# Attention followed by a soft mixture of experts on one core: memory handed from attention to expert weights in eleven steps in place of six, load marks 20 entries later, and a newly written order

## Chip, cores and metric

The kernel runs on one core of a Trainium2 chip. The metric is device time in microseconds (us) of one execution; smaller is better. A stated time is the median of three runs.

## What is computed

All data are float32. The first half is a linear attention with a random-feature map, for 8 batches x 8 heads x 576 tokens of 64 values; the second half is a soft mixture of 8 experts with 4 slots each over the 4608 tokens of 512 values that the first half yields.

```
def phi(x):
    proj = einsum('bhsd,df->bhsf', x, w_phi)            # 64 -> 128 features
    proj = proj - max(abs(proj), axis=-1)
    return concatenate([exp(proj), exp(-proj)], axis=-1)
q_p, k_p = phi(q), phi(k)
kv  = einsum('bhsf,bhsd->bhfd', k_p, v);  z = k_p summed over s
attn = einsum('bhsf,bhfd->bhsd', q_p, kv) / (einsum('bhsf,bhf->bhs', q_p, z) + 1e-6)

x = attn as 4608 x 512;  logits = x @ phi               # 512 -> 32 slots
d = softmax of logits over the 4608 tokens;  slot_input = d.T @ x
slot_out[e] = relu(slot_input[e] @ w1[e]) @ w2[e]       # 512 -> 1024 -> 512, e = 0..7
out = (softmax of logits over the 32 slots) @ slot_out
```

The softmax over tokens needs the logits of every token, so the two expert layers can start only when all of attention is done; the last product needs the outputs of all experts.

## The kernel before, in words

**Stages.** Attention works on 32 head pairs (two batches of one head, 9 tiles of 128 tokens each) and, across them, on 72 blocks of four token tiles. For a block, `proj` multiplies the transposed keys and queries with the feature matrix on TensorE (tiles psk and psq), `kneg_exp`, `kpos_exp`, `qpos` and `qneg` take the exponentials on ScalarE (tiles kf and qf), `kmax` and `qabs` the maxima on VectorE, and `vals` scales the values on GpSimd (tile vs, from the loaded vt). `kvmm` and `kvmid` add up keys by values on TensorE (tile kvp), `kvcopy` takes that to kvs, and `num` multiplies queries with it (tile psn; 96 of them, numbered 0 to 95). `denom`, `recip` and `divide` finish the attention, and every few head pairs the finished tokens are transposed, multiplied with phi and added into the running slot sums. After the last head pair comes a closing part on the last tokens (`fturn`, `flogits`, then the steps whose names begin with z, of which `zsum` reads the last finished tokens, L601), then expert layer 1 (hp, L899), layer 2 (yp, L973), the combination (pso, L993), a copy to o (L997) and 24 stores of 384 KB (L998).

**Loads.** All transfers are issued by SyncE's queue (SP), one after another. There are 37 loads of keys and queries (xs, 512 KB; numbered e, block pair 2e and 2e+1), 32 loads of values (vt, 292.5 KB) and 64 loads of expert weights of 512 KB, called wt0 to wt63: wt0 to wt31 are layer 1, wt32 to wt63 layer 2, and layer 2 works first through wt32 to wt47, then wt48 to wt63. The stores stand behind all loads in the same queue.

**Where weights go.** The left side of the memory holds 30 weight slots from the start (`room`, L50). The pools of attention lie on the right side as a stack; when the pool nearest to the weights has been used for the last time, a step `close` ends it, and a new weight pool of as many slots as then fit is opened and loaded (`opened`, `load_w`). Before the change there are six such ends, listed in `ends`: all three xs buffers after `proj` of block 72, giving slots up to 33; all key and value buffers (kf, vs, vt), up to 38; all query buffers (qf, kvs, and the feature matrix wx), up to 42; the buffers un, xT and xc after that, up to 43, 45 and 51. The other 13 weights, wt51 to wt63, take slots of layer 1 that have been read.

**What holds a load back.** Four things. The queue's order. The buffer's last reader. A depth: `load` ties every load to one sent earlier, `sent[-deep]`, so that it is issued only when that one has landed; deep is 2 in the main part, 3 after one to three ends, then 4. And a mark: `counted` adds up the instructions issued on TensorE and names a matmul as mark each time that the sum passes another 256 entries; a load called with `behind` waits until the last mark that was written before it has been executed.

**Order.** ORDER is a string of one letter per task. The plan takes the letters one by one and emits the task, so the string fixes the order on each of the engines and of the loads on SP at once. `x` is one of the first 30 weights, `b` a load of xs, `a` a load of vt, `c` a `proj`, `m` a `kvmm`, `r` a `num`, `Q` a close.

The lines in which the rules of the loads stand:

```
    seen = [18, 205, None]
    def counted(i, n):
        seen[0] += 1.0107 * n
        if seen[0] >= seen[1]:
            seen[1:] = seen[1] + 256, i.name
    def load(t, x, behind=False):
        i = nc.sync.dma_start(t, x).ins
        ...
        deep = 2 if 8 < len(sent) and len(wpools) < 2 else 3 if 1 < len(wpools) < 5 else 4
```

Of the kernel before, what the change touches and what calls it, by code (L numbers as in the profile page):

```python
# [49 lines left out]
def room(bufs):  # L50

    parts = [bufs["xs"] * XW * 4, bufs["kf"] * 4096 + bufs["vs"] * 2080 + bufs["vt"] * 2368,
             bufs["qf"] * 4096 + 2 * 1056 + 2560, bufs["un"] * 2368, bufs["xT"] * 2048, (bufs["xc"] + 1) * G * DM * 4]
    return [int(n) // 4096 for n in np.cumsum([TOP - sum(parts)] + parts)]


class Plan:
# [44 lines left out]
    "cintAeovfjrhmgpknwlrAvboqmpikwdjfmvwmscdehnticdogafcdjAgphyflarzjihrmgkilrjvpnvobgfqwrAmwvcswlekhdAnAoijlkuyjtcm"
    "mfpnrglphioarmvwdkgqnvjmbxkvwzojeawsAftnocfjlpchAyrrmzdAvbhidvgmlirkmgpwAfwjjqhinosrvwkmntAcAlfvhdeckomdpygmfrjh"
    "wlnvwgqjirpmxvkmiocbzsdejwlfcgaxlbpmntAoAyhqAriknprdczkArAfvvnwfswlAgrjvohwmyzktbidrnrvaojwvhwgivcAfheocwyAAzxlj"
    "mknmdpfAoldpBiVCBgkqjcVjClAsxmrrdnthvmaogiDwvjaxfknhAwEecbiFromgmvpkwyHlpI:jnjqBVCBCGdcsdVtrmDfkKmglEfnooFjhirHL"
    "zhgIvcajwAielbpdcvGwqrmgb:mjfprkmdvjmhiwkKAslntAeyofLnhcfxvigcmpwozArjAhldkflvwgpnboriamdvqhrkcwjngsdbteAicfjmgh"
    "pfllviwjyzojdrrmkgpmAqvwahjknmviwbocecxjdlmnsrgpfdfhgrmkoyAlzajmtpbAArnivvmovhjqwrwkwcksidenoAfAcyjmratJvfMpglhw"
    "jmhnmvlxzwdrqkNgvobmAAwicejpsdyAlipcnfhzlcmoafgrdtqigkdjjhbvnApigfrhklwvwxnstrmAovroicewfjhkpcJAlndjgrmdvmlkopnm"
    "gvwiworjvmayMwzqAyejkcfsdpAcAjxblfxlrmhdmtvghijrpwnrfzvqmkvwnoihmAwkiBogBcVsVCfyhnermjCaAlApadkoDtBivcEgwVnFrrmf"
    "lCobHvwbIqBp:VGCjdcOvDkNhKwnEbdjmoFifzxmgHLGIcj:hgecsfdijmJpAtlyAhdfprKiAzxrkgrlnkLvqawlmnjvvAgrMwhobewpoicsjkcd"  # L110
    "rymnxgbmAotAPflvkndjplvwhrwjrmfimzvAAgwqksaeOcpntojAhicdlfadylvzomJrghvimqkfjhrwpmixbnjwomcfgvAAMxsceAwrltjhkdjm"
    "ikmrdvlyngfobrqpvhmiwgpznavsokjnAmcwweAdtAjaclrxfhyopkmngrirvldwrzoqckfngvfNhjpAwcvxwsAAboitrylvzkhkAvnnrwwvwjAd"
    "gymjxckioAnazledpofchgmAljAOdjBoiCBgmCVmqmrsjpfVrhikdtvawPxfvDAlebpnhcxNmjgwoEimFdBjHlpICgBrVmfv:mkPcwVqybeCfxnl"
    "docpJmbhsrGhfjmzdtvlkignoxKDrqhwrjEimFjmvipHwvLwIcbsedckpO:glnlyAcGofdhiKgMArjtqfAmaLkhgindrbknfhvjawjrgromvjvzw"
    "lAoicpwsdeckymApnAtfzlvojarwxmvhNlrfgwxhkivmJdpjmAOnoqgkwclfnscAAidoetrpbyMrrmlgvvwqjwmkrdhjmgaiNxpfznvkswjnPmhx"
# [944 lines left out]
```

## Time and profile before

| | us |
|---|---|
| median of three runs | 319.07 |
| lowest and highest run | 318.83, 321.95 |
| the profiled execution | 321.82 |
| its span, first to last instruction | 320.0 |
| TensorE matmul busy | 301.3 (94%) |
| VectorE, ScalarE, GpSimd busy | 238.1, 229.3, 150.4 |

The profiled execution is 1.82 us longer than its span, and 2.75 us longer than the median. Every time below that begins with a position, such as "at 264", counts from the start of the span. PE is TensorE's matmuls, PEld its weight loads (which overlap them), DVE VectorE, ACT ScalarE, POOL GpSimd and SPq the queue of SyncE. A wait is put down to what ended it.

### The profile page before, as it was taken

Reading aid. Unit: us, or ns where it says so; the run is one execution under the profiler, and the core shown is the slowest. Engines: PE = TensorE matmul, PEld = TensorE weight load, DVE = VectorE, ACT = ScalarE, POOL = GpSimd, SP = SyncE. Lnnn points to the kernel's source line nnn. Section 1 sums busy time; section 2 is a strip of 40 time slices with the busy share of each in tenths; the row PEclk is TensorE's granted clock in tenths of the full one; section 3 lists DMA queues with packets and bytes.
Section 4 is the critical chain, followed back from the end, with each engine's and each line's share of the span. In section 5 each row is a group of like instructions: output and inputs, shape, how many; then the busy total and the mean of one; then the engine's idle time right before and its main releaser. Section 6 shows DMA issues by size and latency. Waiting matters only on the chain.

```text
span 320.0 us, 17935 instructions
## 1 busy us (share of the span) xinstructions
PE 301.3 (94%) x7736; PEld 255.8 (80%) x7736; DVE 238.1 (74%) x706; ACT 229.3 (72%) x696; POOL 150.4 (47%) x309
## 2 busy tenths in 40 slices
PE   8989999999999999999999999999999999999850
PEld 5989999988889988998899899888989742675520
DVE  2778978897788887787999789898979764424350
ACT  4979997998779896898789889869895521023340
POOL 1655676673357773741777676346686102000000
PEclk9999999999999999999999999999999999999995
DMA  7444475666456464447566656665679899999996
GB/s 237 144 150 142 132 226 173 211 193 193 171 173 201 150 203 136 169 150 212 193 209 237 204 193 218 224 217 160 203 233 297 298 317 363 361 385 376 406 413 267
DMA packets 23119, 73.13 MB, mean 229 GB/s; under 512 B 2560, under 2 KB 2816, under 8 KB 23040
## 3 DMA queue, kind: packets, MB, share of 16 engines
q1 hardware_dynamic: 23040, 71.99, 66.2%
q8 instruction: 61, 1.00, 1.3%
q14 instruction: 18, 0.15, 0.1%
HBM read 62.54 MB, written 9.44 MB: 225 GB/s over the span
## 4 chain that ended last, share of the span: by engine, by line
PE 85%; DMA 4%; DVE 4%; issue 2%; POOL 1%; ACT 0%; DVEq 0%; POOLq 0%; ACTq 0%; SPq 0%
PE psn L179 21%; PE kvp L179 21%; PE psk L179 15%; PE psq L179 6%; PE hp L899 4%; PE yp L973 4%; DMA vt<-vv 2%; PE psl L179 2%; PE psx L182 2%; PE pso L993 2%; DMA wt<-w 2%; PE pss L179 1%; PE psx L764 1%; PE psw L216 1%; POOL vs L314 1%
## 5 line engine op out<-in xcount | busy, mean ns | idle before, releaser
L314 POOL TENSOR_TENSOR vs<-vt,mk 128x520 f32<-128x520 f32 (+3 forms) x96 | 80.0, 839 | 55.6 <-ACT mk L305 31.4
L179 PE MATMUL kvp<-vs,kf 128*64 128x65 f32 (+1 forms) x2560 | 90.2, 223 | 1.0 <-POOL vs L314 1.0
L179 PEld LDWEIGHTS kvp<-vs,kf 128*64 128x64 f32 (+1 forms) x2560 | 82.6, 137 | 8.6 <-issue 5.3
L179 PE MATMUL psn<-kvs,qf 128*64 128x65 f32 x2304 | 80.4, 223 | 2.4 <-issue 1.7
L179 PEld LDWEIGHTS psn<-kvs,qf 128*64 128x64 f32 x2304 | 73.3, 138 | 7.8 <-issue 3.9
L179 PE MATMUL psk<-wx,xs 64*64 64x128 f32 x1120 | 73.8, 274 | 0.0
L179 PE MATMUL psq<-xs,wx 64*64 64x512 f32 x288 | 73.3, 604 | 0.3 <-PE psk L179 0.3
L179 PEld LDWEIGHTS psk<-wx,xs 64*64 64x64 f32 x1120 | 60.0, 133 | 0.7 <-issue 0.7
L301 DVE TENSOR_REDUCE mk<-psk 128x4 f32<-128x512 f32 x72 | 48.4, 678 | 13.7 <-ACT kf L319 8.0
L319 ACT ACTIVATE kf<-psk 128x512 f32<-128x512 f32 x72 | 42.7, 594 | 16.1 <-PE psk L179 7.3
L359 DVE TRANSPOSE_TENSOR_REDUCE mts<-psq 128x16 f32<-128x512 f32 x72 | 50.1, 701 | 2.9 <-PE psk L179 1.1
L364 ACT ACTIVATE qf<-psq 128x512 f32<-128x512 f32 x72 | 42.7, 593 | 2.9 <-PE psn L179 1.5
L322 ACT ACTIVATE kf<-psk 128x512 f32<-128x512 f32 x72 | 42.4, 594 | 1.1 <-DVE mk L301 1.1
L443 POOL TENSOR_TENSOR xc<-un,dn 128x256 f32<-128x256 f32 x62 | 38.1, 616 | 10.7 <-DVE dn L428 8.7
L367 ACT ACTIVATE qf<-psq 128x512 f32<-128x512 f32 x72 | 42.6, 595 | 0.0
L408 DVE TENSOR_TENSOR un<-psn,eq 128x195 f32<-128x195 f32 x96 | 32.7, 346 | 10.1 <-PE psn L179 8.1
L375 ACT ACTIVATE mh<-mts 32x36 f32<-32x36 f32 x128 | 29.3, 229 | 6.3 <-DVE mts L359 5.2
L413 DVE TENSOR_TENSOR un<-psn,un 128x195 f32<-128x195 f32 x96 | 32.7, 352 | 1.5
L381 DVE TENSOR_REDUCE eq<-mh 32x9 f32<-32x36 f32 x128 | 26.3, 205 | 5.2 <-ACT mh L375 3.6
L997 DVE COPY o<-pso 128x384 f32<-128x384 f32 x24 | 12.1, 552 | 15.0 <-PE pso L993 15.0
L973 PEld LDWEIGHTS yp<-wt,sh 128*32 128x32 f32 x512 | 13.7, 110 | 7.6 <-issue 6.8
L973 PE MATMUL yp<-wt,sh 128*32 128x128 f32 x512 | 17.2, 275 | 2.0 <-issue 1.7
(128 smaller groups left out, 309.3 us busy)
## 6 DMA issues: line engine op xcount, KB each, us to landing
wt<-w SPq DMA_DIRECT2D x64, 512.0 KB, 5.1
xs<-xT SPq DMA_DIRECT2D x35, 512.0 KB, 4.2
vt<-vv SPq DMA_DIRECT2D x32, 292.5 KB, 3.5
out<-o SPq DMA_DIRECT2D x24, 384.0 KB, 6.8
xs<-xT SPq DMA_DIRECT2D x2, 256.0 KB, 4.4
wx<-w SPq DMA_DIRECT2D x1, 320.0 KB, 2.8
cs<-cst SPq DMA_DIRECT2D x1, 128.0 KB, 3.9
phs<-phi SPq DMA_DIRECT2D x1, 64.0 KB, 2.8
```

The source lines that it names most:

```text
L179: counted(nc.tensor.matmul(*a, **k).ins, 4)
L301: nc.vector.tensor_reduce(km[b][:, 2], kx[b], axis=AX, op=ALU.max, apply_absolute_value=True)
L314: nc.gpsimd.tensor_tensor(vs[b][:, :, g + t0:g + t1], v[:, t0:t1].unsqueeze(1).broadcast_to([128, 2, n, 65]), km[b][:, 0:2, g + t0:g + t1] ...
L319: nc.scalar.activation(kf[b][:, 1], kx[b], AF.Exp, scale=-1.0)
L322: nc.scalar.activation(kf[b][:, 0], kx[b], AF.Exp)
L359: nc.vector.tensor_reduce(mts.rearrange("p r j -> p j r")[:, o:o + 4], qx[b].rearrange("p j (r t) -> p (j r) t", t=32), axis=AX, op=ALU.ma ...
L364: nc.scalar.activation(qf[b][:, 0], qx[b], AF.Exp)
L367: nc.scalar.activation(qf[b][:, 1], qx[b], AF.Exp, scale=-1.0)
L408: nc.vector.tensor_tensor(un[u][:, CH * c:CH * c + CH], nx[s][:, :, 0], e[:, 1].unsqueeze(2).broadcast_to([128, CH, 65]), op=ALU.mult)
L413: nc.vector.tensor_tensor(x, nx.pop(s)[:, :, 1], x, op=ALU.add)
L443: divider(u).tensor_tensor(x[:, :, h * D:(h + 1) * D], un[u][:, a:b, 0:64], dn[u][:, a:b].unsqueeze(2).broadcast_to([128, b - a, 64]), op= ...
L973: nc.tensor.matmul(yp[q][g:g + 32], sh[e // 4][:, e % 4, c], wt[NE * KC + (q // 2 * NE + e) * 2 + c // 4][:, o:o + COLS], start=(e == 0 an ...
```

## The change

Three things change together. The six pools of attention become eleven, stacked so that each buffer can be given up by itself: the xs buffers one by one (x1 after `proj` of block 69, x2 after block 71, x0, which now also holds the feature matrix, after block 72), the kf buffers one by one (k0, k1), then the rest of keys and values (v), two query buffers (q1, after `num` 92 and 94), then the third with kvs (q2, after `num` 95). The slots after each end are 31, 32, 34, 35, 36, 39, 41, 42 and then 43, 45 and 51 as before. The depth rule follows the number of ends: 2 until the third, 3 until the ninth, then 4; marks hold weights until the third end. The first mark lies at 225 in place of 205, and with it every later one is 20 entries later. And ORDER is a different string, of 1887 letters in place of 1882 (five more ends); the number of each other task is the same.

```diff
-    parts = [bufs["xs"] * XW * 4, bufs["kf"] * 4096 + bufs["vs"] * 2080 + bufs["vt"] * 2368,
-             bufs["qf"] * 4096 + 2 * 1056 + 2560, bufs["un"] * 2368, bufs["xT"] * 2048, (bufs["xc"] + 1) * G * DM * 4]
+    parts = [XW * 4, XW * 4, XW * 4 + 2560, 4096, 4096, 4096 + bufs["vs"] * 2080 + bufs["vt"] * 2368,
+             2 * 4096, 4096 + 2 * 1056, bufs["un"] * 2368, bufs["xT"] * 2048, (bufs["xc"] + 1) * G * DM * 4]
...
-    "bcfbcfdcdklhgdbhilicgndafcjdhomaikjbgjgefmjjplhmrniomfghpmiealdcqjjmfpkhrgmsitdnmlpkvfbgvorqwvjjnrmwcawyszdlhokb"
+    "bcbbcfaffdcdaghghdllcghkinjdiilokdncjdgkmejmqmpjpfsrbmbhonlfjitahrbrifhgkjmjvwcvwivlcoldgneompjmmqpfwrsabfmtcdkh"
...
-    stacks = {k: ExitStack() for k in ("x", "c", "t", "u", "q", "v")}
+    stacks = {k: ExitStack() for k in ("x1", "x2", "x0", "k0", "k1", "v", "q1", "q2", "u", "t", "c")}
...
-    seen = [18, 205, None]
+    seen = [18, 225, None]
...
-        deep = 2 if 8 < len(sent) and len(wpools) < 2 else 3 if 1 < len(wpools) < 5 else 4
+        deep = 4 if len(sent) < 9 else 2 if len(wpools) < 4 else 3 if len(wpools) < 10 else 4
...
-            load(t, wsrc[i], len(wpools) < 2)
+            load(t, wsrc[i], len(wpools) < 4)
...
-        kf[b] = vp.tile([128, 2, 4, 128], F32, tag="kf", name="kf", bufs=BUFS["kf"])
+        kf[b] = kp[b % 3].tile([128, 2, 4, 128], F32, tag="kf", name="kf")
...
-        qf[b] = qp.tile([128, 2, 4, 128], F32, tag="qf", name="qf", bufs=BUFS["qf"])
+        qf[b] = qp[b % 3].tile([128, 2, 4, 128], F32, tag=f"qf{b % 3}", name="qf")
...
-    ends = [("x", [("proj", NB), ("weight", nslot[0] - 1)]),
-            ("v", [("kpos_exp", NB - 1), ("kvmm", len(segs) - 1), ("vals", len(pieces) - 1), ("kvcopy", (NU - 1, 1))]), ("q", [("num", NK - 1)]),
+    kvd = [max((i for i in range(len(segs)) if segs[i][0] == b), default=0) for b in range(NB)]
+    ends = [("x1", [("proj", NB - 3), ("weight", nslot[0] - 1)]), ("x2", [("proj", NB - 1)]), ("x0", [("proj", NB)]),
+            ("k0", [("kpos_exp", NB - 3), ("kvmm", kvd[NB - 3])]), ("k1", [("kpos_exp", NB - 2), ("kvmm", kvd[NB - 2]), ("kvmid", NU - 1)]),
+            ("v", [("kpos_exp", NB - 1), ("kvmm", len(segs) - 1), ("vals", len(pieces) - 1), ("kvcopy", (NU - 1, 1))]),
+            ("q1", [("num", NK - 2), ("num", NK - 4)]), ("q2", [("num", NK - 1)]),
             ("u", [("divide", (NU - 1, 2))]), ("t", [("zlog", c) for c in range(NCH)]), ("c", [("zsum", 4)])]
```

On SP, the place is the last loads of attention and the first weights that go into given-up buffers. In the names, xs and vt are loads of attention, and wt with a number is the weight of that number. Before:

```order
L185 DMA xs_5752<-xT 128x1024
L185 DMA vt_5844<-vv 128x585
L185 DMA wt26_5847<-w1 128x1024
L185 DMA wt27_5876<-w1 128x1024
L185 DMA wt28_5955<-w1 128x1024
L185 DMA wt29_5996<-w1 128x1024
L185 DMA wt30_6062<-w1 128x1024
L185 DMA wt31_6064<-w1 128x1024
L185 DMA wt32_6066<-w2 128x1024
```

and now:

```order
L188 DMA xs_5606<-xT 128x1024
L188 DMA vt_5633<-vv 128x585
L188 DMA vt_5752<-vv 128x585
L188 DMA wt29_5767<-w1 128x1024
L188 DMA wt30_5878<-w1 128x1024
L188 DMA xs_5904<-xT 128x1024
L188 DMA wt31_6035<-w1 128x1024
L188 DMA wt32_6056<-w2 128x1024
L188 DMA wt33_6058<-w2 128x1024
L188 DMA wt34_6177<-w2 128x1024
```

Before, the last xs and vt loads stand ahead of wt26. Now four more weights, wt26 to wt29, and wt30 as a fifth stand ahead of the last xs, xs_5904.

On PE, the place is the last projections of attention: psq and psk together are a `proj`, psq x4 alone is the one of block 72, kvp is `kvmm` and `kvmid`, psn is `num` (x12 for one). Counts are of matmuls, of which each makes two instructions in the trace. Before:

```order
L179 MATMUL kvp<-vs,kf 64x65 x16
L179 MATMUL psq<-xs,wx 64x512 x2
L179 MATMUL psk<-wx,xs 64x128 x8
L179 MATMUL psq<-xs,wx 64x512 x2
L179 MATMUL psk<-wx,xs 64x128 x8
L179 MATMUL kvp<-vs,kf 64x65 x12
L179 MATMUL psn<-kvs,qf 64x65 x12
L179 MATMUL kvp<-vs,kf 64x65 x28
L179 MATMUL psq<-xs,wx 64x512 x4
L179 MATMUL kvp<-vs,kf 64x65 x8
L179 MATMUL psn<-kvs,qf 64x65 x36
```

and now:

```order
L182 MATMUL psn<-kvs,qf 64x65 x36
L182 MATMUL kvp<-vs,kf 64x65 x8
L182 MATMUL psq<-xs,wx 64x512 x2
L182 MATMUL psk<-wx,xs 64x128 x8
L182 MATMUL psq<-xs,wx 64x512 x2
L182 MATMUL psk<-wx,xs 64x128 x8
L182 MATMUL kvp<-vs,kf 64x65 x8
L182 MATMUL psn<-kvs,qf 64x65 x36
L182 MATMUL kvp<-vs,kf 64x65 x8
L182 MATMUL psq<-xs,wx 64x512 x4
L182 MATMUL kvp<-vs,kf 64x65 x16
L182 MATMUL psn<-kvs,qf 64x65 x12
```

Between the projections of blocks 70 and 71 and that of block 72 stand 40 matmuls of kvp and 12 of psn before, and 16 and 36 now; the other matmuls of this stretch have moved behind block 72 or ahead of block 70.

## Rows read from the trace of the kernel before

**Rows 1.** The page: TensorE, then DMA, in 40 slices.
```profile
PEclk9999999999999999999999999999999999999995
DMA  7444475666456464447566656665679899999996
```

**Rows 2.** Stretches: length; PE, PEld, DVE, ACT, POOL busy (instructions); PEclk; DMA share; GB/s.
```profile
8.00:40.00 32.00, 31.02 (x927) 29.63 (x931) 26.21 (x72) 29.17 (x95) 19.51 (x35) 1.00 0.46 142
...
200.00:230.00 30.00, 29.51 (x830) 26.77 (x831) 26.77 (x79) 24.45 (x79) 15.38 (x33) 1.00 0.64 208
230.00:240.00 10.00, 10.00 (x288) 9.05 (x286) 7.92 (x24) 9.46 (x30) 8.20 (x17) 1.00 0.63 205
240.00:250.00 10.00, 10.00 (x243) 9.01 (x243) 8.89 (x32) 5.63 (x15) 4.88 (x14) 1.00 0.92 305
250.00:260.00 10.00, 9.71 (x149) 6.04 (x141) 6.67 (x31) 5.43 (x18) 1.33 (x3) 1.00 0.86 282
260.00:270.00 10.00, 9.82 (x94) 3.82 (x94) 7.04 (x28) 1.62 (x4) 1.33 (x2) 1.00 0.96 356
270.00:280.00 10.00, 10.00 (x156) 5.48 (x152) 3.69 (x19) 0.69 (x1) 0.51 (x1) 1.00 0.98 367
280.00:290.00 10.00, 9.42 (x236) 6.86 (x228) 2.79 (x7) 2.21 (x6) 0.00 (x0) 1.00 1.00 383
290.00:300.00 10.00, 8.56 (x178) 5.33 (x180) 3.60 (x9) 3.25 (x10) 0.00 (x0) 1.00 1.01 388
300.00:310.00 10.00, 8.45 (x134) 4.41 (x124) 6.66 (x15) 5.66 (x15) 0.00 (x0) 1.00 1.03 410
310.00:320.00 10.00, 0.00 (x0) 0.00 (x0) 0.11 (x1) 0.00 (x0) 0.00 (x0) 0.65 0.74 298
```

**Rows 3.** SP's queue in order of time: wt26, wt31, wt32, wt45, wt63.
```profile
231.04 0.33 SPq L185 DMA_DIRECT2D wt<-w  x1
239.82 1.14 SPq L185 DMA_DIRECT2D wt<-w  x1
242.82 0.33 SPq L185 DMA_DIRECT2D wt<-w  x1
264.27 0.33 SPq L185 DMA_DIRECT2D wt<-w  x1
289.60 0.33 SPq L185 DMA_DIRECT2D wt<-w  x1
```

**Rows 4.** SP's waits between 240 and 264: us, times, longest.
```profile
SPq L185 <- DMA wt<-w: 16.0, 12, 3.5
```

**Rows 5.** PE in order of time: block 72, num 95, the last readers of attention.
```profile
238.06 1.09 PE L179 MATMUL psq<-xs,wx 64*64 64x512 f32 x8
248.98 0.92 PE L179 MATMUL psn<-kvs,qf 128*64 128x65 f32 x24
259.13 1.04 PE L601 MATMUL pss<-xc,de 128*32 128x256 f32 x16
```

**Rows 6.** PE at the end: idle time and what ended it, in brackets.
```profile
295.42 1.29 PE L973 MATMUL yp<-wt,sh 128*32 128x128 f32 x38 [0.27 <-DMA wt<-w]
297.81 0.41 PE L973 MATMUL yp<-wt,sh 128*32 128x128 f32 x2 [1.10 <-issue]
306.28 2.94 PE L993 MATMUL pso<-ct,yt 32*128 32x384 f32 x24 [0.77 <-ACT yt L985]
```

**Rows 7.** The page: DMA issues, KB each, us to landing.
```profile
wt<-w SPq DMA_DIRECT2D x64, 512.0 KB, 5.1
xs<-xT SPq DMA_DIRECT2D x35, 512.0 KB, 4.2
vt<-vv SPq DMA_DIRECT2D x32, 292.5 KB, 3.5
out<-o SPq DMA_DIRECT2D x24, 384.0 KB, 6.8
```

**Rows 8.** Waits of all engines: us in total, times, longest.
```profile
POOL vs L314 <- DMA vt<-vv: 7.2, 5, 2.8
```

**Rows 9.** PE's waits between 8 and 250.
```profile
PE psn L179 <- issue: 1.7, 2, 0.9
PE kvp L179 <- POOL vs L314: 1.0, 1, 1.0
```

**Rows 10.** Chain that ended last, two pieces of attention.
```profile
231.44 0.70 PE psn L179 x24
232.13 0.93 PE kvp L179 x32
```

More of the change, by code (lines that the diff above doesn't have):

```diff
@@ L100 @@
 ORDER = (
-    "bcfbcfdcdklhgdbhilicgndafcjdhomaikjbgjgefmjjplhmrniomfghpmiealdcqjjmfpkhrgmsitdnmlpkvfbgvorqwvjjnrmwcawyszdlhokb"
[L102 to L115, printed above, removed]
@@ L116 @@
-    "ocdjocAfliegmhrApmlxAqjtviywkjvdmwmxzAcneloprPgfhAvkiAjrwQnlkpnryzskmnq4pAAtvRovwRywSsSRrSAryrtTvRzzUwyvRSwSyRzS"
-    "ARSvArzwTAyvXRRYzASZwUSQyRAzSAXOXXTY02ZW3oY67Y0WQZ0985W5232QP+535Q67868<o8+9585++Q//=!=!!!")
+    "bcbbcfaffdcdaghghdllcghkinjdiilokdncjdgkmejmqmpjpfsrbmbhonlfjitahrbrifhgkjmjvwcvwivlcoldgneompjmmqpfwrsabfmtcdkh"
+    "yngvgziwehjlmiorjdqgrkvmnvpopfkhjmnAaimsAwcowedclfjydczgpfhbdilmthAjpfarkrbihgrnmqgovuklvwAjjvnrwxwckeioAnysdaop"
+    "fchlbtjzgmrfAvlikdAwmqnrvgAvwhApimjxowmscedlcjkgfmprnyjtbjdvmomhrlqkwifphmgrjcvwaesivwnkazdfpchlbAnxArAkilgrdtyn"
@@ new lines @@
+    "mqmgfovrojwpvhkvjmmswtwnjzcyeflziohoxcrpAdArlAbAirknqmoxvrAkvgwAdscpwftvhnjcxgkiwdorflnavmrjxkdyzwovfAhcgiwclvwA"
+    "gemlnoyjApzbdmAjdknjhpqBoaigfVBmmVrChjsCtrlgAAvkeicwaDpmljvfErhndjFqfimkmrwvnwompHsghbBioI:BtcvVCCwldVxepcDKjyGr"
+    "mkjgjEalbFfqrdvxzAmhnLmvwomHipkfngwIshA:cidfcotjhdxgcGliepKArdlkmnLvorfgwykqlvabJwjjzrvhmwignrspxyezbfcAphAjoicA"
+    "dmfrjgadthigkmpjAmvwlrvlwvxnmofwAjMJcdkhiexcymzqnsmtdlfkAporhlnoigjrqkvAvwArjrnfwgvommahkAwjebpsntcpokdgicrfvjlm"
+    "wbNjvmrxldynwhmvoqwpgfknyhmzcjseicalifzrplfAdaAtAAvrqmwrAsphgbkvoMndtjiAwOcNgbrkdnPmhlvojgirwyfkrvnohzvowAwAvcwd"
@@ new lines @@
+    "jxkycgAzefihlpldimAnmAjBoVBqkCfxCVmghjsrmeipccldntxajpDjmvlawfomEdrhpgqFvkrskixvwnnfAmoohrjwmtvbHI:BGwBcVxCgeiJC"
+    "fyjKpVldzgDhrkiLccvwElFdjHmmIbqfaprAnjmOsdv:bhAmokwfnrGkhrtgJlyiKoAixecgpLcjfvbnovwldmlpjaqzkdrmhingrwvokfwAhsyA"
+    "jcdzgftgAnciejmpfjhvwlrlAbmrpmoqvijvxwdkrwnsokhmcAdayngicMlAefphdgtvlmojjwrrmzknfjNgmbqaAmhoivwpvjsccAiknwedtjgM"
+    "rlmpfhAykmrbdvzonpwlxvrivjqwkgwmfsxmhcilcAenorlfAjdmfytkophAvdbqzriakrAhnpAvwwsocvdwAtcngrjgyolrxvwikjrmfhivwavg"
+    "zwncAeknyzdglAopxAAfolhdbAjkcBjimqVmCpmrjnBfdlgorVksahftgChAmvvrOiwvDwEbBeinPoFjVcCpHBmNVPjImx:dlqCKGLgDamEpsjtj"
@@ L121 @@
+    "kmbcefwhFyniocdplHrIf:bdmrxfxlgvqwhzvGrijmjmmOsKphvkgwcankwneLiolJyofhdcptlAjfMadAzcArivqgPwAkArgmdnkoghnfbvhJpx"
+    "wsirjmvlrjAoitwcvyejcfwpbmNmjhklndaglorfrzOkmdjAvwnvpkwgmcieAhojqliysfjtdzAacnxAomlmfrghdrAMvpkriwpnvmcAwvoqQkhw"
+    "nscojbgyimddzlgrtAvfwjhrvwArekjlinpcgNqmjomkpvQfrQwAsymlnmhizrltqvOsoeARAkpRRjwmSQAynknvSrSPtpwvPQrrTvwyRQwzyRzy"
+    "vwzRASSQRSSzrTUUAvyAzwXRRyAYSZRWoAo4SSzA0X2XTYX37YQ69YZZ80052W25+<365537868Q858Q9+W5+/+/=!!=!!Q")
 COLS = 128
@@ L154, in tile_kernel @@
     up = pool("u", "up", bufs=BUFS["un"], side="right")
-    qp = pool("q", "qp", bufs=2, side="right")
+    qp = [None, None, pool("q2", "q2", bufs=1, side="right")]
+    qp[0:2] = [pool("q1", "q1", bufs=1, side="right")] * 2
     vp = pool("v", "vp", bufs=1, side="right")
-    xp = pool("x", "xp", bufs=1, side="right")
+    kp = [pool(f"k{i}", f"k{i}", bufs=1, side="right") for i in (1, 0)][::-1] + [vp]
+    xp = [pool(f"x{i}", f"x{i}", bufs=1, side="right") for i in (0, 2, 1)]
+    xp = [xp[0], xp[2], xp[1]]
     def xtile(e):
-        return xp.tile([128, XW], F32, tag=f"xs{e % BUFS['xs']}", name="xs")
+        return xp[e % 3].tile([128, XW], F32, tag="xs", name="xs")
     xs, vt, kx, kf, km, vs, kvp, kvs = ({} for _ in range(8))
@@ L206, in tile_kernel @@
     xs[1] = xtile(1)
-    wx = qp.tile([128, 512 + FE], F32, name="wx", bufs=1)
+    wx = xp[0].tile([128, 512 + FE], F32, name="wx")
     wd = wx[:, 512:512 + FE]
@@ L351, in kvcopy @@
         if r == 0:
-            kvs[u] = qp.tile([128, 2, 2, 65], F32, tag="kvs", name="kvs")
+            kvs[u] = qp[2].tile([128, 2, 2, 65], F32, tag="kvs", name="kvs", bufs=2)
         (nc.vector.tensor_copy if d else nc.scalar.copy)(kvs[u][:, :, r], kvp.pop((u, r)))
```

## The prediction

> **What bounds the kernel now.** I read the page first, then a table of stretches, then SP's queue in order of time, then SP's waits, and last PE near the end. The two lines of the page show two regimes [rows 1]: TensorE's clock is at its full level throughout, while the DMA digit lies between 4 and 7 for three quarters of the span and then at 9 to the end. The stretches say it in numbers [rows 2]. Up to 250 PE is busy nearly all the time (31.02 of 32.00 us, 29.51 of 30.00, 10.00 of 10.00) and DMA has a third or more of its time free (shares 0.46 to 0.64 up to 240). From 260 on DMA is at 0.96 to 1.03, and in the last stretch, 310 to 320, the engines do next to nothing while DMA still moves 298 GB/s. So attention is bound by PE, and everything after it by bytes: weights that found no room earlier, and behind them the 24 stores.
>
> How many bytes are late is read from the same rows. The six stretches from 260 to 320 moved (356 + 367 + 383 + 388 + 410 + 298) x 10 us = 22.0 MB. The stores are 24 x 0.393 = 9.4 MB [rows 7]; the other 12.6 MB are 24 weights of 0.524 MB. At 260, then, 24 of the 64 weights were still outside. The queue agrees [rows 3]: wt26 goes out at 231.04, wt31 at 239.82, wt45 at 264.27 and wt63 at 289.60, and the stores begin only behind it. Between 240 and 264 SP waits 16.0 us in 12 waits for an earlier weight to land [rows 4], so in that stretch the depth rule and the transfers pace the queue, not a buffer. The pace from wt31 to wt45 is (264.27 - 239.82) / 14 = 1.75 us each; from wt45 to wt63 it is (289.60 - 264.27) / 18 = 1.41 us.
>
> PE is close behind. In the last 20 us it waits 0.27 us for a weight, 1.10 us for something the trace calls issue, and 0.77 us for ScalarE [rows 6], and its last pso runs until 306.28 + 2.94 = 309.2. If transfers came earlier without limit, PE would allow only a few microseconds.
>
> **The change part by part.** First the earlier ends. In SP's order the last load of attention now stands behind wt30, where before it stood ahead of wt26. So about four weights are issued before the point at which wt26 went out, 231.04. That lead shrinks at once: wt30 and wt31 still wait for marks and with depth 2, and wt32 and wt33 need the xs buffer that block 72 reads, whose projection ends at 238.06 + 1.09 = 239.15 [rows 5]. PE's time between the projections of blocks 70 and 71 and that of block 72 does not change: a kvp instruction takes 0.93 / 32 = 0.029 us, a num 0.70 us [rows 10], so before 80 x 0.029 + 0.70 = 3.0 us, and now 32 x 0.029 + 3 x 0.70 = 3.0 us. I therefore put wt32 at about 239.5 and wt33 at 239.9; before, wt31 went at 239.82 and wt32 at 242.82 [rows 3]. At 240 the new kernel is two weights ahead, not four.
>
> From there three things could hold wt34 to wt44: the depth (3, as before up to wt41), the buffers, or the transfers. The buffers come free in good time: k0, k1 and v with the last kvp, which follows block 72 by a few microseconds, q1 by num 94, ahead of num 95, which ran from 248.98 before [rows 5]. So I let the queue run at its own pace. By the pace of this stretch, wt45 goes out at 239.9 + 12 x 1.75 = 260.9; by the faster pace, 239.9 + 12 x 1.41 = 256.8, but its buffer is read until 259.13 + 1.04 = 260.2 by the last zsum [rows 5], so not before 260.2. Against 264.27 that is 3.4 to 4.1 us earlier. I take 3.8. The largest gain is what the bytes allow: wt45 to wt63 are 19 weights that cannot come before about 260, so 5 of the 24 late ones can be saved, 2.6 MB, and at 22.0 MB in about 56.5 us (0.39 MB/us) that is 6.7 us. The smallest is nothing, if the two weights of lead are lost again.
>
> Behind wt45 nothing new stands in the way: the same 19 weights and 24 stores follow, and DMA is at 1.0 as before. PE does not turn into the bound by this much: stores whose data is ready at 309.2 less the 1.4 us of waits for weights and issue, some 307.8, would still need about 3 us for the last three and some 3 us to the end of the span, 313.8, while 320.0 - 3.8 is 316.2.
>
> Second, the marks. In 200 to 230 PE and PEld start 830 + 831 instructions in 30 us [rows 2], 55 per us, so 20 entries are 0.36 us by which each waiting load goes later. Loads of attention hide that while they have some microseconds in hand. What it may give is the issue idleness of PE, 1.7 us in two waits before psn between 8 and 250 [rows 9], if an instruction page came late there behind a bulk load. The trace doesn't show the cause, so the bounds are 1.7 us of gain and 0.4 us of loss. I take nothing, since PE's later 1.10 us wait for issue [rows 6] came where no mark holds a load.
> The Trainium skill (Runtime: NRT & Kernel Launch, Instruction fetch mechanics) says that an engine's instructions are refilled in blocks of 256 and that crossing a block is mostly hidden; by that rule the shift of the marks gives 0, and by the row at most 1.7 us. The rule speaks against a benefit of this part, and the 0.9 us of the longest such wait are what the trace has against the rule.
>
> Third, the new order. All tasks but the five ends are the same, so PE's work is the same. PE's idle time in the stretches from 8 to 250 is 0.98 in the first row, 0.49 from 200 to 230 and nothing from 230 to 250 [rows 2]; the most that a better order can give in the rows shown is 1.5 us. The price is in the loads. I laid the durations of rows 10 (and 0.93 us for a projection) along both orders and took, for each load, PE's time between its place in the string and the first task that needs it. Most loads of the first third gain lead, but later ones lose it: the values of head pair 24 go from 10.0 to 4.6 us, of 25 from 15.0 to 4.7, of 18 from 5.3 to 3.1, the xs of block 40 from 10.0 to 4.9 and the last xs from 8.8 to 3.0. A vt lands 3.5 us after its issue, an xs 4.2 [rows 7], so these arrive just in time, and the last xs, now behind two weights, is the tightest. In the kernel before, such cases made GpSimd wait 7.2 us in 5 waits for vt [rows 8], of which PE felt 1.0 [rows 9]. I take +0.5 us on PE for this against -0.5 us from the order, zero in sum; PE's delay counts only in part anyway while DMA sets the end.
>
> The sum: 320.0 - 3.8 = 316.2 us of span, 318.0 for the profiled execution with the 1.82 us around it. That execution lies 2.75 us above the median, so on the median the same difference gives 319.07 - 3.8 = 315.3 us.
>
> **The rivals.**
> A. *The lead is lost on the way.* The eleven ends make SP wait for one buffer after another (kf, kf, v, q), and any such wait stalls all loads behind it. For it: depth 3 and the pace stay, the lead at 240 is only two weights. Against it: SP's waits between 240 and 264 are for landings, hardly for engines [rows 4]. If half of the 3.8 us remains, 319.07 - 1.9 = 317.2 us; if nothing, 319.1.
> B. *All five weights are saved and PE gains its idle time.* For it: DMA has free time up to 240 [rows 2]. Against it: depth 3. Time: 319.07 - 6.7 = 312.4 us, about where PE's own end also stops it.
> C. *The later loads of attention come too late, and the kernel is slower.* Place: the values of head pairs 18, 24 and 25 and the last xs. One late vt held GpSimd for up to 2.8 us [rows 8]; if all four hold PE for that long, attention ends 11.2 us later, zsum with it, and wt45 cannot go before 260.2 + 11.2. That is 7.1 us later than the 264.27 of before: 326 us. It decides from 264.27 - 260.2 = 4.1 us of added PE delay, above which the end of attention, not the queue, releases wt45. Against it: PE felt only 1.0 us of GpSimd's waits before [rows 9].
> D. *The change doesn't do what it says*: wt30 and wt31 wait for marks as before and the weights behind them for block 72, so the early ends of xs give nothing, and only kf and q matter. This is the lower half of A and counted there.
>
> **How the numbers follow.** About 1% (3.2 us) is what a measurement of this kernel can tell from no change. The forecast, 2.9 to 5.0 us gained, has 0.50; A 0.27; B 0.10; C 0.13. Faster by over 1%: B and most of the forecast, 0.10 + 0.44 = 0.54. Within 1%: A and the rest of the forecast, 0.33. Slower: C, 0.13. The likeliest case gives 315.3, with a range of its own of 314.1 to 316.2. The range that should hold 8 in 10 reaches down to B with a microsecond of issue time, 311.4, and up past no change with a small part of C, 320.5.
>
> **What would show it.** Right, if in the new trace wt31 goes out some microseconds before block 72 is projected, wt33 near 240, wt45 near 260.5 and wt63 near 286, the stores begin behind it, DMA is at 1.0 from 260 to the end, and the stretch 240 to 260 carries more than the 305 and 282 GB/s of before. Wrong, if SP waits for kvp or psn between 240 and 255 (A), if PE in 100 to 240 shows idle time ended by GpSimd or by xs (C), or if the time went into or out of attention rather than into the transfers after it.

## The result and the profile after

The changed kernel takes 316.36 us (median of 20 runs, 313.87 to 319.27) beside 319.60 us for the kernel before (20 runs, 317.21 to 325.76). The ratio is 0.9902 with a 95% interval of 0.9872 to 0.9931, that is 2.2 to 4.1 us less. Some executions of any of these kernels take a per cent or more longer; ratios and intervals are taken without them, medians with them. The forecast was 315.3 us, 3.8 us less. The profiled execution of the changed kernel has a span of 316.0 us, against 320.0.

The same table of stretches as in [rows 2], for the changed kernel:

```profile
200.00:230.00 30.00, 29.88 (x807) 26.10 (x806) 27.26 (x80) 25.00 (x79) 18.29 (x39) 1.00 0.60 192
230.00:240.00 10.00, 9.39 (x263) 8.26 (x264) 8.59 (x28) 8.23 (x28) 5.34 (x11) 1.00 0.53 175
240.00:250.00 10.00, 9.85 (x243) 8.90 (x241) 7.99 (x30) 5.90 (x16) 6.06 (x17) 1.00 0.93 337
250.00:260.00 10.00, 9.89 (x163) 6.46 (x162) 6.54 (x28) 5.54 (x18) 0.62 (x1) 1.00 0.89 305
260.00:270.00 10.00, 10.00 (x99) 3.84 (x93) 7.23 (x28) 1.61 (x4) 0.97 (x2) 1.00 0.99 358
270.00:280.00 10.00, 10.00 (x148) 5.24 (x144) 3.69 (x19) 0.69 (x1) 0.88 (x1) 1.00 1.00 370
280.00:290.00 10.00, 9.39 (x242) 6.79 (x230) 2.63 (x6) 2.08 (x5) 0.00 (x0) 1.00 0.97 353
290.00:300.00 10.00, 10.00 (x208) 6.28 (x204) 4.38 (x9) 3.88 (x10) 0.00 (x0) 1.00 0.93 362
300.00:310.00 10.00, 7.23 (x110) 3.87 (x106) 6.23 (x13) 5.25 (x13) 0.00 (x0) 0.98 1.02 397
310.00:316.00 6.00, 0.00 (x0) 0.00 (x0) 0.00 (x0) 0.00 (x0) 0.00 (x0) 0.50 0.62 245
```

The reader is to see two things. Between 240 and 260 DMA carries 337 and 305 GB/s instead of 305 and 282, so weights moved ahead. And between 280 and 300 DMA is no longer full (0.97 and 0.93, where it was 1.00 and 1.01 before), while PE is busy for all of 290 to 300 instead of 8.56 us of it: the two have come level.

SP's queue in order of time, changed kernel: wt31; wt32 and wt33 in one row; wt42; wt43; wt45; wt63 (compare [rows 3]).

```profile
235.58 0.33 SPq L188 DMA_DIRECT2D wt<-w  x1
...
238.38 0.81 SPq L188 DMA_DIRECT2D wt<-w  x2
...
252.12 0.94 SPq L188 DMA_DIRECT2D wt<-w  x1
...
256.84 0.33 SPq L188 DMA_DIRECT2D wt<-w  x1
...
259.69 0.33 SPq L188 DMA_DIRECT2D wt<-w  x1
...
285.51 0.33 SPq L188 DMA_DIRECT2D wt<-w  x1
```

wt45 goes out 4.6 us earlier (264.27 before) and wt63 4.1 us earlier (289.60 before). At 240, two more weights are out than before (wt33, against wt31). What held SP between 240 and 262 in the changed kernel (us, times, longest):

```profile
SPq L188 <- DMA wt<-w: 9.1, 8, 1.7
SPq L188 <- DVE xT L557: 3.2, 1, 3.2
SPq L188 <- PE pss L604: 2.0, 1, 2.0
SPq L188 <- PE kvp L182: 1.2, 1, 1.2
```

It now waits for buffers too, which it hardly did before [rows 4]: for xT between wt42 and wt43, and for the last zsum (pss) ahead of wt45. A landing was what wt45 waited for before, and it went out 2.7 us after layer 1 had begun; now it goes out 2.2 us ahead of layer 1 (259.69 against 261.92), as soon as attention lets go of its buffer. The same 2.2 us stand in all eight profiled runs of the new order with eleven ends. The queue has caught up with the end of attention: wt45 to wt50, which share that buffer, can start earlier only if attention ends earlier.

PE in order of time, changed kernel: the first instruction of layer 1, and the last pso.

```profile
261.92 0.64 PE L905 MATMUL hp<-wt,phs 128*32 128x512 f32 x4
...
305.06 2.94 PE L999 MATMUL pso<-ct,yt 32*128 32x384 f32 x24 [0.77 <-ACT yt L991]
```

Attention and its closing part did not get shorter in this execution: layer 1 starts at 261.92, before at 261.55. All of the gain lies behind that point: from there to the end of the span it is 316.0 - 261.92 = 54.1 us, and was 320.0 - 261.55 = 58.5 us. The last pso ends at 308.0 (309.2 before [rows 6]), and from there to the end it is 8.0 us instead of 10.8. I use the first of these lengths below and call it the stretch after attention.

### The profile page after: what moved, and what is told of

Read it like the earlier page. It is cut to its first block, busy times and chain, and to the rows that moved or that the text cites. A ratio compares the mean times of both kernels' runs of the same rounds, so it can differ in the third digit from the quotient of the medians.

```text
span 316.0 us, 17950 instructions
## 1 busy us (share of the span) xinstructions
PE 301.7 (95%) x7736; PEld 256.3 (81%) x7736; DVE 240.1 (76%) x706; ACT 229.7 (73%) x696; POOL 149.6 (47%) x309
## 4 chain that ended last, share of the span: by engine, by line
PE 84%; DVE 5%; ACT 3%; issue 3%; DMA 2%; POOL 1%; SPq 0%; DVEq 0%; ACTq 0%
PE kvp L182 21%; PE psn L182 20%; PE psk L182 14%; PE psq L182 6%; PE yp L979 5%; PE hp L905 4%; PE pso L999 3%; PE psl L182 3%; PE psx L185 2%; DMA xs<-xT 2%; PE pss L182 2%; PE psx L767 1%; DVE mts L362 1%; PE pss L604 1%; ACT mh L378 1%
## 5 line engine op out<-in xcount | busy, mean ns | idle before, releaser
L182 PE MATMUL psk<-wx,xs 64*64 64x128 f32 x1120 | 71.6, 274 | 0.0
L182 PEld LDWEIGHTS psk<-wx,xs 64*64 64x64 f32 x1120 | 59.1, 133 | 0.6 <-issue 0.6
L322 ACT ACTIVATE kf<-psk 128x512 f32<-128x512 f32 x72 | 42.9, 598 | 14.0 <-PE psk L182 6.2
L325 ACT ACTIVATE kf<-psk 128x512 f32<-128x512 f32 x72 | 43.1, 600 | 0.0
L1003 ACT COPY o<-pso 128x384 f32<-128x384 f32 x24 | 10.3, 483 | 12.5 <-PE pso L999 11.4
L182 PEld LDWEIGHTS psq<-xs,wx 64*64 64x64 f32 x288 | 15.5, 133 | 4.1 <-issue 0.8
```

The lines of the kernel that those rows point to most:

```text
L182: counted(nc.tensor.matmul(*a, **k).ins, 4)
L325: nc.scalar.activation(kf[b][:, 0], kx[b], AF.Exp)
```

## Experiments

Each kernel was timed beside the kernel before; ratios are to it, with a 95% interval. Layer 1 begins, and the stretch after attention is taken, in one profiled execution each, so these scatter by a microsecond or two.

| kernel | order | marks | ends | ratio (interval) | layer 1 begins | stretch after |
|---|---|---|---|---|---|---|
| before | old | 205 | 6 | 1 | 261.55 | 58.5 |
| e6 | old | 225 | 6 | 0.9994 (0.9962 to 1.0027) | 259.18 | 60.0 |
| e7 | old | none | 6 | 1.0105 (1.0057 to 1.0153) | 261.76 | 58.2 |
| e2 | old | 205 | 11 | 0.9964 (0.9905 to 1.0023) | 258.43 | 55.9 |
| e12 | old | 225 | 11 | 0.9994 (0.9957 to 1.0030) | 259.01 | 59.6 |
| e1 | new | 225 | 6 | 0.9924 (0.9886 to 0.9962) | 259.90 | 56.8 |
| changed | new | 225 | 11 | 0.9902 (0.9872 to 0.9931) | 261.92 | 54.1 |
| e5, the same again | new | 225 | 11 | 0.9903 (0.9873 to 0.9934) | 258.77 | 54.3 |
| e3 | new | 205 | 11 | 1.0057 (1.0008 to 1.0105) | 262.51 | 56.0 |
| e9 | new | 205, four loads free | 11 | 0.9963 (0.9926 to 1.0000) | 263.71 | 54.1 |
| e10 | new | 225, weights only | 11 | 0.9958 (0.9921 to 0.9995) | 259.04 | 53.6 |
| e4 | new | none | 11 | 0.9888 (0.9812 to 0.9963) | 260.32 | 53.5 |
| e11, depth 4 | new | 225 | 11 | 0.9909 (0.9879 to 0.9940) | 261.51 | 54.7 |
| e8, 13 weights left out | new | 225 | 11 | 0.9845 (0.9797 to 0.9894) | 260.91 | 52.8 |

**e1: the new order with six ends.** The file before, with `seen = [18, 225, None]` and the new string without the five added closes:

```diff
-    seen = [18, 205, None]
+    seen = [18, 225, None]
...
-    "bcfbcfdcdklhgdbhilicgndafcjdhomaikjbgjgefmjjplhmrniomfghpmiealdcqjjmfpkhrgmsitdnmlpkvfbgvorqwvjjnrmwcawyszdlhokb"
+    "bcbbcfaffdcdaghghdllcghkinjdiilokdncjdgkmejmqmpjpfsrbmbhonlfjitahrbrifhgkjmjvwcvwivlcoldgneompjmmqpfwrsabfmtcdkh"
```

> The changed kernel's new order and later marks, with the six ends and the depth rule of before. Theory 1 (the ends make the room that the order's four weights of lead need): wt30 to wt32 wait for block 72 at about 238, wt33 to wt37 for the last kvp at about 245, wt38 to wt41 for num 95 at about 250.5; wt45 goes out at 261.5 to 264 and most of the gain is lost: 318 to 319.5 us, ratio to before 0.995 to 1.00. Theory 2 (the new order alone moves the weights, the ends only spread them): wt45 within 0.5 us of 259.7, time within 0.8 us of the changed kernel, ratio 0.988 to 0.993.

Measured 0.9924, 317.63 us. By the ratios most of the gain is there without the new ends, on the side of theory 2. But its stretch after attention is 2.7 us longer than that of the changed kernel, and SP's waits, of the kind that theory 1 has, say why. Between 236 and 250, e1:

```profile
SPq L185 <- PE kvp L179: 9.4, 3, 4.3
SPq L185 <- DMA wt<-w: 2.8, 2, 1.9
```

and the changed kernel in the same stretch:

```profile
SPq L188 <- DMA wt<-w: 6.7, 5, 1.7
SPq L188 <- PE kvp L182: 4.0, 2, 2.8
```

With six ends SP waits 9.4 us for PE's kvp, hence for buffers that are given up together, with eleven ends 4.0 us. So the ends, with the depth rule that comes with them (the two were not taken apart), shorten the wait that they are made for. The lead that this gives lasts up to wt45. In e1 wt45 waits for the landing of an earlier weight:

```profile
260.03 0.33 SPq L185 DMA_DIRECT2D wt<-w  x1
```

That is 0.1 us after its layer 1 began, against 2.2 us ahead of it in the changed kernel. What it is worth in the median, 0.9902 against 0.9924, lies inside the intervals.

**e2 and e12: eleven ends with the old order**, marks at 205 and at 225. The diff of the pools, depth rule and ends is that of the change; the string is the old one with its first three Q replaced by eight, each behind the last reader of its buffers:

```diff
-    stacks = {k: ExitStack() for k in ("x", "c", "t", "u", "q", "v")}
+    stacks = {k: ExitStack() for k in ("x1", "x2", "x0", "k0", "k1", "v", "q1", "q2", "u", "t", "c")}
...
-    seen = [18, 205, None]
+    seen = [18, 225, None]
```

(The second pair of lines in e12 only.)

> The kernel before with the eleven ends and the new depth rule alone; its order of tasks and its marks stay, each end is written as soon as its last readers are written. Theory 1 (ends and order need each other): the order still holds wt26 to wt29 until 231 to 238, so wt31 goes out no earlier than 239; wt45 at 262 to 264, ratio 0.993 to 1.00. Theory 2 (order alone): ratio 0.998 to 1.003, the same as before. A third possibility, that the ends alone do it: ratio 0.988 to 0.992.

> The kernel before with eleven ends, the new depth rule and marks at 225: everything of the change but the order. If ends and order each shorten the stretch after attention and add up (58.5 us before, 55.9 with ends alone, 56.8 with the order alone, 54.1 with both): here 55.5 to 56.5 us from the first hp to the end of the span, ratio to before 0.991 to 0.997. If the ends give something only with the new order: 58 us or more, ratio 0.998 to 1.002. If the new order costs attention more than it saves: ratio below 0.990, better than the changed kernel.

Measured 0.9964 and 0.9994; both intervals hold 1. The 55.9 us of e2 was one execution, its shortest run (316.09 us, while its median is 322.03); e12 gives 59.6 us, so the expected adding up is not there, and e12 is as its second possibility says. That the ends give something only where the order brings weights early enough to need them is the reading that fits e1, e12 and the changed kernel. SP in order of time, e12, wt63:

```profile
288.04 0.33 SPq L188 DMA_DIRECT2D wt<-w  x1
```

That is 29.0 us after its layer 1 began (28.05 before, 23.6 in the changed kernel): in this execution the weights of the old order are as late as ever.

**e3: the changed kernel with the marks at 205.**

```diff
-    seen = [18, 225, None]
+    seen = [18, 205, None]
```

> The changed kernel with the marks at 205 again, 20 entries earlier. If the marks are worth nothing, as I forecast: ratio to before 0.990 plus or minus 0.003 and PE's waits for issue between 8 and 250 within 1 us of the changed kernel's 2.4 us. If the later marks keep bulk loads off instruction pages: PE's waits for issue rise to 4 us or more and the ratio to 0.994 or above.

Measured 1.0057, 322.32 us: slower than the kernel before, and 1.55% or some 5 us slower than the changed kernel, by 20 entries. But PE's waits for issue did not rise; other waits did. PE's waits between 8 and 250, e3:

```profile
PE kvp L182 <- POOL vs L317: 3.0, 4, 1.6
PE psn L182 <- issue: 0.7, 1, 0.7
```

GpSimd in order of time, e3 near 135, then PE near 186:

```profile
134.54 0.62 POOL L317 TENSOR_TENSOR vs<-vt,mk 128x260 f32<-128x260 f32 x1 [4.68 <-DMA vt<-vv]
```

```profile
185.96 1.15 PE L182 MATMUL kvp<-vs,kf 128*64 128x65 f32 x32 [1.61 <-POOL vs L317]
```

In the changed kernel PE has no wait for GpSimd in this list at all. By their place in the order these are the values of head pairs 18 and 24, two of those that the prediction named as just in time; the four waits are two for head pair 18 (1.0 us), one for 24 (1.6) and one for 28 (0.5), which it did not name. Near 186 the chain is visible on SP: the load goes out at 181.48 in e3,

```profile
181.48 0.33 SPq L188 DMA_DIRECT2D vt<-vv  x1
```

and at 179.87 in the changed kernel:

```profile
179.87 0.77 SPq L188 DMA_DIRECT2D vt<-vv  x1
```

The 20 entries are 0.36 us, yet moving marks *earlier* made this load 1.6 us *later*. The reason is in the code: a load waits for the last mark that was written ahead of it. Where a load stands in the string just behind a mark at 205 but ahead of the same mark at 225, the earlier setting binds it to one mark later, a whole step of 256 entries. Counting the entries along the string gives eight such loads in the new order: xs 12 and 28, the values of head pairs 27 and 28, and the weights wt7, wt8, wt15 and wt21. (The expectation of e9 below knows only the first four; weights wait for marks too until the third end.) Every load behind them on SP waits with them. xs 27 and xs 28 in e3:

```profile
164.77 0.33 SPq L188 DMA_DIRECT2D xs<-xT  x1
...
173.16 0.33 SPq L188 DMA_DIRECT2D xs<-xT  x1
```

and in the changed kernel:

```profile
166.71 0.33 SPq L188 DMA_DIRECT2D xs<-xT  x1
...
171.12 0.33 SPq L188 DMA_DIRECT2D xs<-xT  x1
```

xs 27 is on no edge, and xs 28 follows it after 8.4 us instead of 4.4: 4.0 us more, not far from the 4.7 us that 256 entries take at the prediction's 55 per us. The depth of 2 then hands the delay on, from xs 28 to wt22 and from wt22 to the values of head pair 24.

**e9: four loads free of marks.** The test of that reason:

```diff
-    seen = [18, 225, None]
+    seen = [18, 205, None]
...
-        load(xs[e], xT[e - 1], e > 4)
+        load(xs[e], xT[e - 1], e > 4 and e not in (12, 28))
...
-        load(vt[u], vv[u // H, u % H], u > 1)
+        load(vt[u], vv[u // H, u % H], u > 1 and u not in (27, 28))
```

> The changed kernel with the marks at 205, but four loads wait for no mark: xs 12 and 28, the values of head pairs 27 and 28. These are the loads that stand in the written order between a mark at 205 and the same mark at 225, so that with 205 each waits for one mark later, a whole step of 256 entries, some 4 to 5 us. If that step is why 205 was slow in this order: ratio to before 0.988 to 0.995, PE without the 1.6 us wait for GpSimd near 186. If it is the 20 entries by which all other loads go earlier: 1.002 to 1.009 as with 205 alone.

Measured 0.9963: between the two expectations, 0.9 points better than e3 and 0.6 worse than the changed kernel, with 0.3 to 0.5 points of uncertainty on each ratio. The wait near 186 is gone. PE's waits between 8 and 250, e9:

```profile
PE psn L182 <- issue: 2.0, 4, 0.7
PE kvp L182 <- issue: 0.8, 1, 0.8
PE kvp L182 <- POOL vs L317: 0.6, 2, 0.4
```

So the four loads account for roughly half of what the marks at 205 cost, and the rest stays open. The four weights on the edge were still tied here. One of them, wt15, stands two places ahead of the values of head pair 18, and these are about as late as in e3. wt14 to wt16 in one row, the values of head pair 18, and GpSimd's wait for them, e9:

```profile
125.96 6.28 SPq L188 DMA_DIRECT2D wt<-w  x3
134.87 0.33 SPq L188 DMA_DIRECT2D vt<-vv  x1
...
137.95 0.62 POOL L317 TENSOR_TENSOR vs<-vt,mk 128x260 f32<-128x260 f32 x1 [4.35 <-DMA vt<-vv]
```

and the two loads in the changed kernel:

```profile
126.30 4.19 SPq L188 DMA_DIRECT2D wt<-w  x3
131.56 0.33 SPq L188 DMA_DIRECT2D vt<-vv  x1
```

No run freed these weights, so what they cost is not shown; PE's waits for GpSimd in e9 come to 0.6 us only. Here the waits for issue have grown to 2.8 us in five, where e3 had one, but the changed kernel's profiled execution had 2.4 us too.

**e6 and e7: the old order with marks at 225, and with none.**

```diff
-        if behind and seen[2]:
+        if False:
```

(This is e7; e6 only sets 225 in place of 205.)

> The kernel before with the marks at 225 and nothing else. Theory M (a mark at 205 itself costs time, in any order, since it releases bulk loads at a bad moment): ratio to before 0.985 to 0.993. Theory O (the marks at 205 hurt only the new order, which has its later loads of attention late): ratio 0.997 to 1.003.

> The kernel before with no load waiting for a mark. Theory M: as fast as the marks at 225 or faster, ratio 0.985 to 0.993. Theory O: 0.996 to 1.003. If marks protect instruction pages in the old order: above 1.003.

Measured 0.9994 and 1.0105. In the old order the 20 entries are worth nothing, as theory O says. Yet eight loads stand on an edge there too (xs 12, 25 and 29, the values of head pairs 13, 18, 23 and 26, and wt9). The values of head pair 18 go out 8.7 us behind the load ahead of them with the marks at 205 and 5.5 us with 225, and PE waits for GpSimd near there in neither. This fits theory O, by which standing on an edge costs something only where a load has little lead in hand; the lead itself was not varied. No marks cost 1% in the old order, which is the third possibility of e7. Its profile shows waits of PE for issue of 1.3 us between 8 and 262, against 1.7 before, so those waits don't show as the cause. The profiled execution of e7 is its shortest (321.74 us), that of before is 2.2 us above its median (321.82), so the two profiles can't show the 1%; it stays open.

**e4 and e10: the new order with no marks, and with marks for weights only** (e10). e4 has the edit of e7, e10 this:

```diff
-        load(xs[e], xT[e - 1], e > 4)
+        load(xs[e], xT[e - 1])
...
-        load(vt[u], vv[u // H, u % H], u > 1)
+        load(vt[u], vv[u // H, u % H])
```

> The changed kernel with no load waiting for a mark; order, buffers and depth stay. If instruction pages do not suffer under bulk loads (crossing a block is hidden): PE's waits for issue stay near 2.4 us, loads go out a little earlier, ratio to before 0.986 to 0.991. If pages come late behind bulk loads: many more waits of PE for issue, 6 us or more between 8 and 250, attention ends later by as much, ratio 0.995 to 1.02.

> The changed kernel with marks for weights only; loads of xs and vt wait for buffers, depth and their turn. If late loads of attention cost the changed kernel time: attention ends earlier on the mean, ratio to before 0.982 to 0.988. If not, 0.988 to 0.992, as the changed kernel; above 0.995 if loads of attention now hit instruction pages.

Measured 0.9888 and 0.9958. Without any marks the new order is as fast as with them at 225, within a wide interval; PE's waits for issue were 1.0 us, no more than with marks. Freeing only the loads of attention did not help. So late loads of attention cost the changed kernel nothing that this can see, and no value of the marks themselves shows in the new order. That what counts is the moment at which a few tight loads are let go is argued from e3 and e9.

**e8: what is left behind the transfers.** The last 13 weights are not loaded, and layer 2 reads what lies in their slots, so 6.8 MB less have to come:

```diff
             i = len(wt)
+            if i >= nslot[-1]:
+                wt.append(wt[order[i - nslot[-1]]])
+                continue
```

> The changed kernel without the loads of the last 13 weights (wt51 to wt63); layer 2 reads what lies in those slots. It shows what is left behind the transfers. If the bytes still bound the end as before: 6.8 MB at 0.39 MB/us, 17 us, time near 300 us. If PE's production of outputs is now as close as I said (end of the last pso at 308.0 in the changed kernel, at most 1 us earlier without weights, and some 5 us from there to the end): 1.5 to 4 us less than the changed kernel, ratio to before 0.977 to 0.987.

Measured 0.9845, 314.7 us: only about 1.8 us less than the changed kernel, 0.57% of 319.6, and with four runs this is known to about 2 us. Stretches, e8:

```profile
270.00:280.00 10.00, 10.00 (x176) 5.94 (x172) 3.70 (x19) 0.69 (x1) 0.00 (x0) 1.00 0.03 11
280.00:290.00 10.00, 10.00 (x250) 7.13 (x244) 3.56 (x8) 3.02 (x8) 0.00 (x0) 1.00 0.42 162
290.00:300.00 10.00, 10.00 (x224) 6.36 (x224) 4.88 (x11) 4.16 (x11) 0.00 (x0) 1.00 0.89 345
300.00:310.00 10.00, 4.71 (x54) 2.16 (x44) 4.72 (x11) 3.94 (x11) 0.00 (x0) 0.88 1.02 398
```

and its last pso:

```profile
302.54 2.94 PE L1002 MATMUL pso<-ct,yt 32*128 32x384 f32 x24 [0.77 <-ACT yt L994]
```

DMA stands idle from 270 to 280 (share 0.03), PE is busy without a gap to 300, and from the end of the last pso, 305.5, to the end of the span it is 8.2 us, as in the changed kernel (8.0). So the weights hold up the stretch after attention of the changed kernel by only 54.1 - 52.8 = 1.3 us; the rest is PE's way from layer 1 to the outputs, and the stores behind it. The stores are bytes too: with no weights in the way DMA is full again from 300 to 310 (1.02). e8 tests the weights alone; no run left out stores.

**e11: depth 4 from the third end.**

```diff
-        deep = 4 if len(sent) < 9 else 2 if len(wpools) < 4 else 3 if len(wpools) < 10 else 4
+        deep = 4 if len(sent) < 9 else 2 if len(wpools) < 4 else 4
```

> The changed kernel with a depth of 4 from the third end on, in place of 3 up to the ninth. If the pace of SP between 240 and 256 still held weights back: wt45 no earlier than its buffer allows, but all before it landed, wt63 at 284 to 285 in place of 285.5, ratio to before 0.986 to 0.989. If attention's end and the outputs now set the time: 0.989 to 0.992, no change from the changed kernel.

Measured 0.9909, the same as the changed kernel, though wt63 goes out another 3.2 us earlier:

```profile
282.35 0.33 SPq L188 DMA_DIRECT2D wt<-w  x1
```

This agrees with e8: weights that come still earlier find PE and the stores in the way.

**e5: the changed kernel once more,** the same file.

> The changed kernel once more, beside the two that follow. Expected 0.990 of the kernel before, plus or minus 0.004. If its advantage over the marks at 205 was a matter of the chip of that day, it comes out at 0.995 or above here.

Measured 0.9903. Its profiled execution is 2.9 us shorter than the first one (span 313.1 against 316.0), and all of that lies ahead of layer 1, which begins at 258.77 instead of 261.92. What differs there is PE's waiting for issue, 2.4 us in three waits in the first execution and none in the second. The longest, stretch 42 to 46, first execution and then e5:

```profile
42.00:46.00 4.00, 2.83 (x94) 2.69 (x94) 2.19 (x6) 2.67 (x9) 1.06 (x1) 1.00 0.66 236
```

```profile
42.00:46.00 4.00, 4.00 (x136) 3.95 (x136) 3.23 (x10) 3.12 (x11) 1.06 (x1) 1.00 0.67 211
```

No version that does the whole work beats the changed kernel beyond the intervals: e4 (0.9888) and e11 (0.9909) are level with it.

## Why the prediction was right, and where it was not

**What bounds the kernel: right.** Attention by PE, and the rest by late bytes. With the same attention (261.55 and 261.92 in the profiled executions) the span fell by 4.0 us.

**The weights: right in place and nearly in size.** The steps were two weights of lead at 240, wt45 at 260.2 to 260.9, 3.4 to 4.1 us gained. Measured: two weights, wt45 at 259.69, 4.4 us less in the stretch after attention. The stores, which ran 10.8 us behind the last pso and now 8.0, gave 2.8 us of it, and PE (first hp to the end of the last pso: 47.7 us before, 46.1 now) the other 1.6 us. But little of PE's part was waiting for weights. PE's waits behind 262, before:

```profile
PE yp L973 <- issue: 1.7, 2, 1.1
PE yp L973 <- DMA wt<-w: 0.3, 1, 0.3
```

and in the changed kernel, where no wait for a weight is left:

```profile
PE pso L999 <- issue: 0.6, 1, 0.6
```

Issue gave 1.1 us of the 1.6 and weights 0.3. Issue in this stretch also varies without the change (0.2 us in e6, 1.5 in e7), so that part can't be put down to it. The waits for weights can: they are 2.8 us in e6 and 1.9 in e12, both with the old order, and nothing in any run with the new one.

The time of wt45 came out right by its bound and not by the pace. The pace of 1.75 us per load did not hold, from wt33 (238.76) to wt42 (252.12) it was 1.48 us. SP then stood until 256.84 for xT, and the last zsum released wt45, which is the 260.2 of the prediction. That 260.9, by a pace that did not hold, lay so near was luck.

**Which part of the change does it: half right.** The prediction put the lead down to SP's order and the room to the ends, and took both together. Taken apart, the order with the later marks gives 0.9924, the ends alone nothing (0.9994, 0.9964), and the ends on top of the order 0.2 points that the intervals don't separate. The buffer waits of e1, 9.4 us against 4.0, show the ends at work, and their lead is still there at wt45, which in e1 waits for a landing and not for the last zsum. In profiled executions that is 2.5 to 2.7 us of the stretch after attention (56.8 against 54.1 and 54.3), in the ratios 0.2 points, some 0.7 us; which of the two is nearer to what the ends are worth is open.

**The marks: the step that failed.** "I take nothing" for the 20 entries, within -1.7 and +0.4 us. In the old order it holds (0.9994). In the new one the same 20 entries are worth 1.0057 to 0.9902, some 5 us, and without them the change would have been slower than the kernel before. I had sized the shift as 0.36 us for each waiting load; the runs showed in its place that a mark is a step, and that a load on the edge of it moves by the whole step (4.0 us for xs 28). Roughly half is shown to come from four of eight such loads (e9); the other half is open. So the sum of zero for the marks and the order came out right by luck: nothing in the prediction looked at how the marks fall in the new order, and with 225 PE happened to wait for none of its tight loads.

The Trainium skill (Runtime: NRT & Kernel Launch, Instruction fetch mechanics) has the refill of instructions mostly hidden, and by that rule the marks would save PE no waits for issue. The runs agree in part: without marks the new order has no more issue waits (e4, 1.0 us). But 2.4 us of such waits in one execution and none in another of the same kernel (e5) are not hidden here; that they are late pages is argued in the last section, not shown.

**The new order's lost leads: right as a danger, not in the sum.** I had taken +0.5 us against -0.5. In the changed kernel PE waits for no late value. With the marks at 205 it waits four times (3.0 us in all, 2.6 of it on head pairs named in the prediction), so rival C was real and near, with 3.0 us of PE delay rather than 11.2, and a time of 322 us rather than 326. Its margin was wrong too: it allowed PE 4.1 us of delay before the end of attention, and not the queue, would release wt45. In the changed kernel the end of attention already does, so no margin is left, and the prediction's "PE's delay counts only in part" no longer holds there.

**PE as the next bound: right, but mis-sized.** I allowed 6 us from the last pso to the end; it is 8.0 to 8.4 us in every run of the new order with eleven ends. As far as weights go, the floor is therefore near e8's 314.7 us and not 312.4, and rival B was out of reach. Rival A did not come: its sign, SP waiting for kvp between 240 and 255, is there with 1.2 us only. SP's waits for buffers between 240 and 262 came to 6.4 us, 5.2 of it after 252, and the lead was kept.

The total of 3.1 us is smaller than the 4.4 us of the profiled stretch. If attention ended about a microsecond later in the changed kernel on the mean, this would be explained, but single executions scatter by 3 us there, so it is argued, not shown.

## What to carry to other kernels

Where a transfer phase follows a compute phase, count the bytes that are still outside when the phases meet and divide by the rate of the full stretch; then look how far behind the engine stands, for that is all that can be won. Giving buffers up piecemeal can pay only if something is already waiting for them in the queue. And a load that is tied to sparse marks moves in whole steps: after any change of order, list the loads that stand just behind a mark, and among them those with less lead in hand than a step.

## What I had not expected

- A shift of 20 entries, 0.36 us, changed the time by some 5 us in one order (1.0057 to 0.9902) and by nothing in another (0.9994), though eight loads stand on an edge in either.
- Dropping all marks cost 1% in the old order (1.0105) and nothing in the new (0.9888).
- PE's waits for issue look like late instruction pages. In the changed kernel's trace an instruction packet begins at about 42.6, 117.8 and 228.3, and PE goes on at 44.87, 120.66 and 230.61, each 2.3 to 2.9 us later, after 1.17, 0.55 and 0.69 us of idling. But such packets begin every 4.5 us on the mean through all of attention, mostly without a wait, so this is a likeness and not a proof. The waits come and go between executions of one kernel, 2.4 of the 2.9 us by which its two spans differ (316.0 and 313.1).
- Taking away 6.8 MB of transfers in the end stretch, which DMA filled to 0.93 to 1.02, was worth only 1.8 us: a full DMA share doesn't say that those bytes set the end, when an engine behind them is as busy.
